# Attention with decay and a gated product on one core: rows of two heads moved by TensorE instead of DMAs in the first four chunks

## The chip, the cores and the metric

The kernel runs on one core of one Trainium2 chip. The metric is the device time in microseconds (us) of one execution. Three runs of the kernel before gave 395.66, 395.9 and 396.56 us, a median of 395.9.

The engines are TensorE (PE; its weight loads are shown as PEld), VectorE (DVE), ScalarE (ACT), GpSimd (POOL) and SyncE (SP), which issues DMAs. Results of PE land in eight PSUM banks.

## The reference

```python
# r, k, v, w: (B=4, H=8, S=768, D=48); u: (H, D)
for t in range(S):
    cur = einsum('bhd,bhe->bhde', u * k[:, :, t], v[:, :, t])
    y[:, :, t] = einsum('bhd,bhde->bhe', r[:, :, t], state + cur)
    state = w[:, :, t, :, None] * state + einsum('bhd,bhe->bhde', k[:, :, t], v[:, :, t])
x = y.transpose(0, 2, 1, 3).reshape(B, S, H * D)
h = maximum(x @ w_in, 0)                      # 384 -> 1024
conv = conv_w[0] * h(t-1) + conv_w[1] * h(t) + conv_w[2] * h(t+1)
out = (h * sigmoid(conv)) @ w_out             # 1024 -> 384
```

The inputs r, k, v, w and u are float32; the three weights of the second part are float64.

## The kernel before

**Tiling.** The sequence of each of the four batches is cut into six chunks of 128 steps, so there are 24 chunks n = 0 to 23, with c = n mod 6. The 384 rows of x are kept transposed in `xT`, as three tiles of 128 partitions, and a high and a low part of each value, so that fast float32r products keep the precision. Three tiles hold eight heads of 48 rows thus: of each tile, rows 0 to 47 and 64 to 111 are a pair of heads, and rows 48 to 63 and 112 to 127 take sixteen rows each of heads 6 and 7. The gaps of the first six heads thus hold the last two heads in three pieces.

**Stage a of a chunk** (`stage_a`) transposes w, k and r on PE with the identity (L517), after an ACT copy that puts heads 6 and 7 into the gaps (L511). Two scans on DVE (L524, L531) make running products of w, and L529 and L535 multiply k and r into them; the result `kr` has k in part 0 and r in part 1. Scores and outputs of heads 6 and 7 need these heads on rows of their own, in `last`: six DMAs on SP's queue (L539) copy sixteen partitions each from `kr` to `last`. POOL makes z = r k u (L543, L545), DVE sums it (L546) and POOL puts the sum on a diagonal (L549). `kback` (L557) transposes k back.

**Stage b** (`stage_b`) makes the scores (L607: for six heads from `kr`, for heads 6 and 7 from `last`), copies their upper half into `pm` (L611), makes the new state (L624, L628), and the outputs: what the state carries (L635, with the decayed state `sd` of L591 and L594 spread by ACT into `sbd`, L599) and what lies within the chunk (L645). ACT and DVE write the outputs as high and low part to `xT` (L651, L653). Heads 6 and 7 land in a spare slot of `xT`; for the chunks c = 3 and c = 5 six DMAs (L662) copy their rows, for all chunks since the last such copy, to the gaps.

**The weights** come in pieces: a DMA load on SP's queue (L455 and L459 for w_in, L470 for w_out), then DVE, ACT and POOL turn float64 into a high and a low float32 part (L419 to L440).

**The blocks.** A block is 384 steps of a batch. For each of eight groups of 128 columns, PE makes x @ w_in (L673), ACT and DVE the gating (L685 to L694), POOL the low part (L695), and PE the output product (L702). A block can start once the chunks that it reads have all rows of their outputs in `xT`; the first block reads chunks 0 to 3.

**The order.** The instructions are not written in the order in which they run. Each step is given to a planner (`Plan.op`) with its engine, a modelled length (`LEN`), what it reads and writes, and a rank. `Plan.issue` goes through modelled time: whenever an engine is free, it takes the ready step with the lowest rank. The order that results is fixed for each engine, and engines run in order on the chip. Loads of chunk n have rank 14 n - 10, its stage a 14 n, its stage b 14 n + 7; the first block starts at rank 56 and its groups are 5 apart; the weight pieces are 4 apart, w_in from 10, w_out from 60. DMAs use one queue, SP's; the planner models what they move.

**The head.** Fourteen products of zeros (L331, `WARM`) run on PE while the first loads are under way. POOL makes the constants and broadcasts u over 128 partitions with one DMA of its own queue (L347).

Of the kernel before, what the change touches and what calls it, by code (L numbers as in the profile page):

```python
# [19 lines left out]
W_LO, W_HI = 0.75, 1.05  # L20
BANKS = 8
GH = 5
WARM = 14

CHUNK, LEAD, UNIT, DOWN, PIECE = 14.0, 0.0, 5.0, 1.6, 4.0
FIRST_IN, FIRST_OUT = 10.0, 60.0
AHEAD, GUARD = 10.0, 10.0
SPREAD = (3, 5)


LEN = dict(
# [2 lines left out]
    stt=0.54, gate=0.47, wts=0.47, wstt=0.47,  # L34
    fill=0.25, kh=0.42, guard=0.72, sbd=0.34, xhi=0.49, relu=0.5, mul=0.49, sig=0.43, cast=0.42, out=0.37, exp=0.52,
    z=0.98, diag=1.07, lo=0.97,
    load=0.55, issue=0.45, spread=0.6,
)
TAIL = dict(PE=0.22, DVE=0.11, ACT=0.13, POOL=0.07, SP=2.2)

# [65 lines left out]
class Plan:  # L106
# [29 lines left out]
    def issue(self):  # L136
        n = len(self.ops)
        left = [len(o[3]) for o in self.ops]
        users = [[] for _ in range(n)]
        for i, o in enumerate(self.ops):  # L140
            for d in o[3]:
                users[d].append(i)
        engines = ("PE", "DVE", "ACT", "POOL", "SP")
        ready = {e: [] for e in engines}
        free = dict.fromkeys(engines, 0.0)
        locked = dict(DVE=0.0, POOL=0.0)
        wire = Wire(("SP", "ACT"))
        for i in range(n):
            if not left[i]:
                ready[self.ops[i][0]].append((self.ops[i][7], i))  # L150
        events, order, t = [], [], 0.0

        def places(bufs):
            taken = []
            for b in bufs:
                if b.t is None:
                    if b.turn == b.kind.served:
                        b.t = b.kind.take()
                    if b.t is None:
                        for x in reversed(taken):  # L160
                            x.kind.places.insert(0, x.t)
                            x.kind.held -= 1
                            x.kind.served -= 1
                            x.t = None
                        return False
                    taken.append(b)
            return True

        while len(order) < n:
            for e in engines:  # L170
                if free[e] > t:
                    continue
                for k, (_, i) in enumerate(sorted(ready[e])):
                    if places(self.ops[i][4]):
                        break
                else:
                    continue
                ready[e].remove((self.ops[i][7], i))
                _, us, _, _, _, moves, port, _ = self.ops[i]
                at = t  # L180
                if port:
                    other = "POOL" if e == "DVE" else "DVE"
                    at = max(t, locked[other])
# [12 lines left out]
            todo = []  # L196
            while events and events[0][0] <= t + 1e-9:
                todo.append(heapq.heappop(events)[1])
            for i in todo:
                if i < 0:  # L200
                    continue
                for b in self.ops[i][4]:
                    b.uses -= 1
                    if not b.uses:
                        b.kind.held -= 1
                        b.kind.places.append(b.t)
                for u in users[i]:
# [81 lines left out]
def rwkv_conv_moe_kernel(  # L289
# [35 lines left out]
    banks = [ps.tile([P, 512], F32, name=f"bank{i}") for i in range(BANKS)]  # L325


    idle = fconst.tile([P, HB], BF16, name="idle")
    nc.vector.memset(idle, 0.0)
    for _ in range(WARM):  # L330
        nc.tensor.matmul(banks[-1][:, 0:HB], lhsT=idle[:, 0:P], rhs=idle, start=True, stop=True)  # L331

# [11 lines left out]
    nc.gpsimd.affine_select(out=upper, in_=ones_f, pattern=[[1, P]], compare_op=ALU.is_gt,  # L344
                            fill=0.0, base=0, channel_multiplier=-1)
    ubc = fconst.tile([P, H, D], F32, name="ubc")
    nc.gpsimd.dma_start(out=ubc, in_=u.rearrange("h d -> (h d)").partition_broadcast(P))  # L347
    cw = const.tile([P, 3, FT], F32, name="cw")
    one_end = fconst.tile([P, WID], F32, name="one_end")
    nc.vector.memset(one_end, 0.0)  # L350
# [30 lines left out]
    kr_k = kind("kr", 3, [P, 2, WID], fill=lambda t: nc.gpsimd.memset(t[:, :, 0:WID:WID - 1], 0.0))  # L381
    last_k = kind("last", 2, [R, 2, SL + 1], fill=lambda t: nc.gpsimd.memset(t, 0.0))
    sbd_k = kind("sbd", 2, [R, NP, R], fill=lambda t: nc.gpsimd.memset(t, 0.0))
    z_k = kind("z", 1, [P, H, D])
    dg_k = kind("dg", 2, [P, H])
    pm_k = kind("pm", 2, [P, 2, NP, L])
    junk_k = kind("junk", 1, [P, H, D], BF16)
    kh_k = kind("kh", 2, [P, NP, R], fill=lambda t: nc.gpsimd.memset(t[:, KT], 0.0))
    sd_k = kind("sd", 2, [R, NP, D])
    s_k = kind("s", 2, [R, NP, D])  # L390
# [89 lines left out]
    def loads(n):  # L480
# [3 lines left out]
        for nm, src in (("w", w), ("k", k), ("r", r), ("v", v)):  # L484
            op("SP", "load", lambda nm=nm, src=src: nc.sync.dma_start(  # L485
                out=st[nm].t[:, :, 0:D], in_=src[b, :, s, :].rearrange("h t d -> t h d")), [], [st[nm]], moves=1.15)

    def seg(t, at):

        return t[:, 0:KT * SL].rearrange("p (m s) -> p m s", s=SL)[:, :, at:at + L] if at == 0 else \  # L490
            t[:, at - 1:at - 1 + KT * SL].rearrange("p (m s) -> p m s", s=SL)[:, :, 1:1 + L]
# [4 lines left out]
    def thirds(t):  # L496
        return t[:, 0:KT * L].rearrange("p (m t) -> p m t", t=L)
# [4 lines left out]
    def stage_a(n):  # L502
# [7 lines left out]
        def tr(src, t, cols):  # L510
# [4 lines left out]
            def f():  # L515
                for m in range(KT):
# [17 lines left out]
        tr(R_, rp, lambda m: rp.t[:, m * L:(m + 1) * L])  # L534
        op("DVE", "kt", lambda: nc.vector.tensor_tensor(out=seg(kr.t[:, 1], 0), in0=thirds(rp.t), in1=seg(kr.t[:, 1], 0),  # L535
                                                        op=ALU.mult), [rp], [(kr, 1)], [kr])
        for g in range(2):
            for m in range(KT):
                op("SP", "spread", lambda g=g, m=m: nc.sync.dma_start(  # L539
                    out=last.t[64 * g + 16 * m:64 * g + 16 * m + 16],  # L540
                    in_=kr.t[64 * g + D:64 * g + 64, :, m * SL:m * SL + SL + 1]), [kr, (kr, 1)], [(last, g, m)], [last],
                    moves=0.05)
        op("POOL", "z", lambda: nc.gpsimd.tensor_tensor(out=z.t, in0=R_.t[:, :, 0:D], in1=K_.t[:, :, 0:D], op=ALU.mult),  # L543
           [R_, K_], [z], port=True)
        op("POOL", "z", lambda: nc.gpsimd.tensor_tensor(out=z.t, in0=z.t, in1=ubc, op=ALU.mult), [], [z], port=True)  # L545
        op("DVE", "dg", lambda: nc.vector.tensor_reduce(  # L546
            out=dg.t.rearrange("p (g m) -> p m g", g=2), in_=z.t.rearrange("p (m g) d -> p m g d", g=2), axis=AX.X,
            op=ALU.add), [z], [dg])
# [20 lines left out]
    def stage_b(n):  # L569
# [13 lines left out]
        def place(m):  # L583

            at = (m + odd) % NP
            return slice(at * L, (at + 1) * L)

        if c:
            sd, sbd = Buf(sd_k), Buf(sbd_k)
            old = chunks[n - 1]["s"]  # L590
            op("DVE", "sd", lambda: nc.vector.tensor_tensor(  # L591
                out=sd.t[:, 0:KT], in0=old.t[:, 0:KT], in1=kr.t[0:R, 0, 1:WID:SL].unsqueeze(2).to_broadcast([R, KT, D]),
                op=ALU.mult), [old, kr], [sd], port=True)
            op("DVE", "small", lambda: nc.vector.tensor_scalar(  # L594
                out=sd.t[:, KT], in0=old.t[:, KT], scalar1=last.t[:, 0, 1:2], scalar2=None, op0=ALU.mult),
                [old, *lasts], [(sd, 1)], [sd, last], port=True)
            for g in range(2):
                p = slice(64 * g, 64 * g + D)
                op("ACT", "sbd", lambda g=g, p=p: nc.scalar.copy(out=sbd.t[p, :, 64 * g:64 * g + D], in_=sd.t[p]),  # L599
                   [sd, (sd, 1)], [sbd] if g == 0 else [(sbd, 1)], [sbd])  # L600
        sc = [Buf(pb), Buf(pb)]

        def scores():
# [10 lines left out]
        if c < NCH - 1:  # L614
# [14 lines left out]
            else:  # L629
                op("DVE", "s", lambda: nc.vector.tensor_copy(out=s.t, in_=tv()[0:R]), [t], [s])  # L630
        y = Buf(pb)
        if c:
            def carried():
                for m in range(NP):
                    nc.tensor.matmul(y.t[0:R, place(m)], lhsT=sbd.t[:, m, :], rhs=rt(m),  # L635
                                     start=(m == 0), stop=False, skip_group_check=True)
            op("PE", "carried", carried, [sbd, (sbd, 1), kr, (kr, 1), *lasts], [y], [last])
# [8 lines left out]
                                     rhs=pm.t[:, g, m, :], start=(c == 0 and m == 0), stop=True,  # L646
                                     skip_group_check=True)
        op("PE", "y", within, [vN, pm, (pm, 0), (pm, 1)], [y])
        ts = slice(1 + c * L, 1 + (c + 1) * L)
        slots = slice(KT * odd, KT * odd + NP)  # L650
        op("ACT", "xhi", lambda: nc.scalar.copy(out=xT[0:R, slots, 0, ts], in_=pairs(y.t)),  # L651
           [y], [("x", odd, c, 0), ("spare", c)])
# [102 lines left out]


    piece = iter([FIRST_IN + PIECE * j for j in range(3 * KT)] + [FIRST_OUT + PIECE * j for j in range(FT)])
    for f0 in range(0, DF, HB):
        plan.rank = FIRST_IN + PIECE * KT * (f0 // HB)
        win_pieces(f0, min(HB, DF - f0), piece)  # L760
        if f0 == 0:
            load_conv()
# [58 lines left out]
```

## Time and profile before

| | |
|---|---|
| three runs, median | 395.9 us (395.66 to 396.56) |
| profiled execution | 397.97 us, of which span 396.3 us |
| PE busy | 353.8 us (89%), 2704 matmuls |
| DVE busy | 279.9 us (71%) |
| ACT busy | 231.6 us (58%) |
| POOL busy | 173.3 us (44%) |
| granted clock of PE, mean | 0.921 |
| DMA | 35.43 MB, mean 89 GB/s; 106640 of 118124 packets under 512 B |
| copies to `last` (L539) | 144 DMAs, 16.2 KB each, median 1.9 us to landing |

The span is the time from the first to the last instruction of the profiled execution. In the strips, the span is cut into forty equal slices, and each digit is the busy share in tenths (PEclk: the clock granted to PE, in tenths of the full one). A row of the timeline has the start and the length of a group of instructions in us, engine, line and operation, the tile written and the tiles read, and, in brackets, the idle time before it and what ended it. SPq is the issuing of DMAs on SP's queue. A line of a helper function can carry several shapes.

### The profile page before, as it was taken

The page shows a single profiled execution, that of the slowest core. Times are in us where ns is not written, and L with a number is a line of the kernel's source. Part 1 is how long each engine was busy: PE and PEld are TensorE (multiplying, and loading weights), DVE is VectorE, ACT ScalarE, POOL GpSimd, SP SyncE. Part 2 cuts the span into 40 slices and gives each one's busy share as a digit, 9 for nine tenths or more (in the row PEclk, how much of TensorE's full clock was granted, in tenths as well). Part 3 has the DMA queues.
Part 4 walks back from the last instruction along what each step waited for, and adds up shares of the span by engine and source line. Part 5 has one row for each costly group of instructions (what it writes and reads, how often), then busy time and mean ns, then how long its engine had stood idle before and what let it go on. Part 6 is the DMA issues. An engine that isn't in the chain of part 4 may idle for free.

```text
span 396.3 us, 7712 instructions
## 1 busy us (share of the span) xinstructions
PE 353.8 (89%) x2704; PEld 320.5 (81%) x2704; DVE 279.9 (71%) x575; ACT 231.6 (58%) x597; POOL 173.3 (44%) x191
## 2 busy tenths in 40 slices
PE   6672485797899999999999999999999999999991
PEld 3561274686888899999899999889899999999991
DVE  4557867879998768678866885688778755746510
ACT  3234445249996666269856663686767526656711
POOL 5418576457774443235554342255444321332320
PEclk9568556679999999999999999999999999999997
DMA  8899996559344254395406443743444221010101
GB/s 151 133 114 153 159 219 168 98 129 120 68 82 91 51 87 88 75 157 90 95 27 110 81 91 72 128 85 84 77 84 86 51 48 54 2 41 22 40 0 66
DMA packets 118124, 35.43 MB, mean 89 GB/s; under 512 B 106640, under 2 KB 115088, under 8 KB 118080
## 3 DMA queue, kind: packets, MB, share of 16 engines
q1 hardware_dynamic: 118016, 34.69, 47.3%
q8 instruction: 23, 0.38, 0.4%
q0 software_dynamic: 64, 0.20, 0.2%
q14 instruction: 21, 0.17, 0.2%
HBM read 25.39 MB, written 4.72 MB: 76 GB/s over the span
## 4 chain that ended last, share of the span: by engine, by line
PE 69%; DMA 10%; DVE 9%; SPq 4%; ACT 3%; issue 2%; POOL 2%; DVEq 0%; POOLq 0%; ACTq 0%
PE bank L702 24%; PE bank L673 21%; PE bank L645 5%; DMA gh<-in_moe_w_in_dram 5%; PE bank L607 5%; PE bank L517 5%; PE bank L635 5%; DMA r<-in_r_dram 4%; SPq L485 3%; PE bank L624 3%; PE bank L557 2%; DVE a L687 1%; DVE a L689 1%; DVE g L692 1%; DVE bank L419 1%
## 5 line engine op out<-in xcount | busy, mean ns | idle before, releaser
L673 PE MATMUL bank<-xT,wi 128*128 128x386 f32 x576 | 127.1, 347 | 2.2 <-DVE val L430 2.2
L702 PE MATMUL bank<-wo,gh 128*128 128x384 f32 x576 | 125.0, 343 | 1.2 <-POOL gh L695 1.2
L695 POOL TENSOR_TENSOR gh<-g,gh 128x384 fp32r<-128x384 f32 x64 | 64.7, 1015 | 122.1 <-ACT gh L694 120.5
L673 PEld LDWEIGHTS bank<-xT,wi 128*128 128x128 f32 x576 | 100.0, 189 | 6.0 <-DVE val L430 2.5
L702 PEld LDWEIGHTS bank<-wo,gh 128*128 128x128 f32 x576 | 100.5, 188 | 2.4 <-POOL gh L695 1.6
L687 DVE SCALAR_TENSOR_TENSOR a<-bank,cw,a 128x384 f32<-128x384 f32 x64 | 38.5, 609 | 14.9 <-ACT a L686 14.8
L691 ACT ACTIVATE a<-a 128x384 f32<-128x384 f32 x64 | 33.3, 522 | 22.5 <-DVE a L689 22.4
L692 DVE TENSOR_TENSOR g<-bank,a 128x384 f32<-128x384 f32 x64 | 34.5, 548 | 16.0 <-ACT a L691 16.0
L611 DVE COPY_PREDICATED pm<-upper,bank 128x512 f32<-128x512 int32 x48 | 33.8, 731 | 12.1 <-PE bank L607 11.9
L685 ACT ACTIVATE bank<-bank 128x386 f32<-128x386 f32 x64 | 30.4, 478 | 17.8 <-PE bank L673 16.7
L549 POOL TENSOR_SCALAR_AFFINE_SELECT pm<-dg 128x1024 f32<-128x1024 f32 x24 | 26.3, 1094 | 33.0 <-PE bank L645 26.8
L694 ACT CAST gh<-g 128x384 fp32r<-128x384 f32 x64 | 32.4, 513 | 13.2 <-DVE g L692 12.9
L689 DVE SCALAR_TENSOR_TENSOR a<-bank,cw,a 128x384 f32<-128x384 f32 x64 | 38.6, 611 | 0.8
L686 ACT ACTIVATE a<-bank,cw 128x384 f32<-128x384 f32 x64 | 36.6, 582 | 0.3
L543 POOL TENSOR_TENSOR z<-r,k 128x384 f32<-128x384 f32 x24 | 24.3, 1013 | 27.0 <-DMA r<-in_r_dram 26.9
L524 DVE TENSOR_TENSOR_SCAN kr<-bank,one_end 128x387 f32<-128x387 f32 x24 | 23.0, 957 | 15.6 <-PE bank L517 15.6
L653 DVE TENSOR_TENSOR xT<-bank,xT 112x512 fp32r<-112x512 f32 x24 | 16.5, 688 | 20.3 <-ACT xT L651 20.1
L645 PE MATMUL bank<-pm,v 128*48 128x128 f32 (+1 forms) x384 | 28.3, 294 | 0.0
L651 ACT CAST xT<-bank 112x512 fp32r<-112x512 f32 x24 | 14.2, 592 | 23.8 <-PE bank L645 23.7
L645 PEld LDWEIGHTS bank<-pm,v 128*48 128x48 f32 (+1 forms) x384 | 21.9, 133 | 5.7 <-issue 3.7
L557 PE MATMUL bank<-ident,kr 128*128 128x128 f32 x72 | 13.9, 308 | 13.5 <-DVE kr L529 13.5
L607 PEld LDWEIGHTS bank<-kr 48*128 48x128 f32 x288 | 20.8, 214 | 6.4 <-issue 4.8
(84 smaller groups left out, 522.8 us busy)
## 6 DMA issues: line engine op xcount, KB each, us to landing
w<-in_w_dram SPq DMA_DIRECT2D x24, 192.0 KB, 3.9
k<-in_k_dram SPq DMA_DIRECT2D x24, 192.0 KB, 4.5
r<-in_r_dram SPq DMA_DIRECT2D x24, 192.0 KB, 4.7
v<-in_v_dram SPq DMA_DIRECT2D x24, 192.0 KB, 3.0
out_dram<-val SPq DMA_DIRECT2D x24, 192.0 KB, 2.0
last<-kr SPq DMA_DIRECT2D x144, 16.2 KB, 1.9
gh<-in_moe_w_out_dram SPq DMA_DIRECT2D x2, 1152.0 KB, 6.6
gh<-in_moe_w_in_dram SPq DMA_DIRECT2D x4, 432.0 KB, 8.2
```

The lines of the kernel that those rows point to most:

```text
L607: nc.tensor.matmul(sc[g].t[:, m * L:(m + 1) * L], lhsT=kt(m)[p], rhs=rt(m)[p], start=True, stop=True)
L611: op("DVE", "cp", lambda g=g: nc.vector.copy_predicated(out=pm.t[:, g], mask=upper.unsqueeze(1).to_broadcast([P, NP, L]), data=sc[g].t.rea ...
L645: nc.tensor.matmul(y.t[rows, cs], lhsT=vf[:, h * D:h * D + rows.stop - rows.start], rhs=pm.t[:, g, m, :], start=(c == 0 and m == 0), stop= ...
L673: nc.tensor.matmul(t.t[:, 0:xs.stop - xs.start], lhsT=wi[:, m, a, f * P:(f + 1) * P], rhs=xT[:, x0 + m, c, xs], start=(m == 0 and j == 0), ...
L686: ("ACT", "mul", lambda: nc.scalar.mul(out=a(), in_=h(1), mul=cw[:, 1, f:f + 1]), [t, "cw"], [a1]),
L687: ("DVE", "stt", lambda: nc.vector.scalar_tensor_tensor(out=a(), in0=h(0), scalar=cw[:, 0, f:f + 1], in1=a(), op0=ALU.mult, op1=ALU.add), ...
L689: ("DVE", "stt", lambda: nc.vector.scalar_tensor_tensor(out=a(), in0=h(2), scalar=cw[:, 2, f:f + 1], in1=a(), op0=ALU.mult, op1=ALU.add), ...
L691: ("ACT", "sig", lambda: nc.scalar.activation(out=a(), in_=a(), func=AF.Sigmoid), [], [a1]),
L692: ("DVE", "gate", lambda: nc.vector.tensor_tensor(out=g.t[:, 0:width], in0=h(1), in1=a(), op=ALU.mult), [t, a1], [g]),
L694: ("ACT", "cast", lambda: nc.scalar.copy(out=part(0)[:, 0:width], in_=g.t[:, 0:width]), [g], [key]),
L695: ("POOL", "lo", lambda: nc.gpsimd.tensor_tensor(out=part(1)[:, 0:width], in0=g.t[:, 0:width], in1=part(0)[:, 0:width].bitcast(F32), op=AL ...
L702: nc.tensor.matmul(acc.t[:, 0:DM], lhsT=part(a)[:, tt * P:(tt + 1) * P], rhs=wo[:, f, c, :], start=(f == 0 and a + c == 0), stop=(f == FT ...
```

## The change

In chunks 0 to 3 (`n < EARLY`), six matmuls with selection matrices `sel` bring the rows of heads 6 and 7 of `kr` into one PSUM bank, and one ACT copy writes them to `last`; the six DMAs are left out there. Also in these chunks, the outputs of heads 6 and 7 are made by PE at their final rows: v of these heads is copied by ACT into a zero-padded `vx`, the decayed state into `sbx`, and the products run over three tiles instead of four pairs. `xT` is written in its final place, and the six DMAs after chunk 3 of the first batch are left out.

u is loaded as one row by SP and broadcast by a product with a row of ones; the second z step now waits for it. `WARM` goes from 14 to 10. The planner counts PE's steps as 1.4 times as long before its time 60 (`COLD`), and a small DMA as 0.64 instead of 0.6.

```diff
-WARM = 14
+WARM = 10
...
+EARLY = 4
+COLD = 60.0
...
+                if e == "PE" and t < COLD:
+                    us *= 1.4
...
-    nc.gpsimd.dma_start(out=ubc, in_=u.rearrange("h d -> (h d)").partition_broadcast(P))
+    sel = fconst.tile([P, KT, R], F32, name="sel")
+    nc.gpsimd.memset(sel, 0.0)
+    for g in range(2):
+        for m in range(KT):
+            nc.gpsimd.tensor_copy(out=sel[:, m, 64 * g + 16 * m:64 * g + 16 * m + 16], in_=ident[:, 64 * g + D:64 * g + 64])
...
+    sbx_k = kind("sbx", 1, [R, KT, P], fill=lambda t: nc.gpsimd.memset(t, 0.0))
+    vx_k = kind("vx", 1, [P, KT, 2, 64], fill=lambda t: nc.gpsimd.memset(t, 0.0))
...
+    def spread_u():
+        t, row = Buf(pa), Buf(val_k)
+        op("SP", "issue", lambda: nc.sync.dma_start(out=row.t[0:1, :], in_=u.rearrange("h d -> (h d)").unsqueeze(0)),
+           [], [row], moves=0.05)
+        op("PE", "gather", lambda: nc.tensor.matmul(t.t[:, 0:H * D], lhsT=ones_f[0:1, :], rhs=row.t[0:1, :],
+                                                    start=True, stop=True), [row], [t])
+        op("ACT", "kh", lambda: nc.scalar.copy(out=ubc.rearrange("p h d -> p (h d)"), in_=t.t[:, 0:H * D]), [t], ["ubc"])
...
+        if n < EARLY:
+            gt = Buf(pa)
+            both = 2 * (SL + 1)
+
+            def gather():
+                for a in range(2):
+                    for m in range(KT):
+                        nc.tensor.matmul(gt.t[0:R, a * (SL + 1):(a + 1) * (SL + 1)], lhsT=sel[:, m, :],
+                                         rhs=kr.t[:, a, m * SL:m * SL + SL + 1], start=(m == 0), stop=(m == KT - 1))
+            op("PE", "gather", gather, [kr, (kr, 1)], [gt])
+            op("ACT", "kh", lambda: nc.scalar.copy(out=last.t.rearrange("p a t -> p (a t)"), in_=gt.t[0:R, 0:both]),
+               [gt], [(last, 0, 0)], [last])
+        else:
...
+        early = n < EARLY
+        if early:
+            vx = Buf(vx_k)
+            op("ACT", "fill", lambda: nc.scalar.copy(
+                out=vx.t[:, :, :, D:64], in_=vN.t[:, 2 * KT:H].rearrange("p g (m i) -> p m g i", m=KT)), [vN], [vx])
...
+                    op("ACT", "sbd", lambda g=g, p=p: nc.scalar.copy(
+                        out=sbd.t[p, 0:KT, 64 * g:64 * g + D], in_=sd.t[p, 0:KT]),
+                        [sd], [sbd] if g == 0 else [(sbd, 1)], [sbd])
+                    op("ACT", "fill", lambda g=g, p=p: nc.scalar.copy(
+                        out=sbx.t[p, :, 64 * g + D:64 * g + 64], in_=sd.t[p, KT].rearrange("p (m i) -> p m i", m=KT)),
+                        [(sd, 1)], [sbx] if g == 0 else [(sbx, 1)], [sbx, sd])
...
+                def carried_rows():
+                    for m in range(KT):
+                        nc.tensor.matmul(y.t[:, m * L:(m + 1) * L], lhsT=sbx.t[:, m, :], rhs=rt(KT),
+                                         start=(m == 0), stop=False, skip_group_check=True)
+                    for m in range(KT):
+                        nc.tensor.matmul(y.t[0:R, m * L:(m + 1) * L], lhsT=sbd.t[:, m, :], rhs=rt(m),
+                                         start=False, stop=False, skip_group_check=True)
...
+            def within_rows():
+                for m in range(KT):
+                    for g in range(2):
+                        nc.tensor.matmul(y.t[64 * g:64 * g + 64, m * L:(m + 1) * L], lhsT=vx.t[:, m, g, :],
+                                         rhs=pm.t[:, g, KT, :], start=(c == 0 and m == 0), stop=False,
+                                         skip_group_check=True)
+                for m in range(KT):
+                    for g in range(2):
+                        nc.tensor.matmul(y.t[64 * g:64 * g + D, m * L:(m + 1) * L], lhsT=vN.t[:, 2 * m + g, :],
+                                         rhs=pm.t[:, g, m, :], start=False, stop=True, skip_group_check=True)
+            op("PE", "y_rows", within_rows, [vx, vN, pm, (pm, 0), (pm, 1)], [y])
+            op("ACT", "kh", lambda: nc.scalar.copy(out=xT[:, 0:KT, 0, ts], in_=thirds(y.t)), [y], [("x", odd, c, 0)])
+            op("DVE", "kt", lambda: nc.vector.tensor_tensor(
+                out=xT[:, 0:KT, 1, ts], in0=thirds(y.t), in1=xT[:, 0:KT, 0, ts].bitcast(F32), op=ALU.subtract),
+                [y, ("x", odd, c, 0)], [("x", odd, c, 1)])
+            return
...
+    plan.rank = -AHEAD + 1
+    spread_u()
```

More of the change, by code (lines that the diff above doesn't have):

```diff
@@ L36 @@
     z=0.98, diag=1.07, lo=0.97,
-    load=0.55, issue=0.45, spread=0.6,
+    gather=1.6, carried_rows=1.4, y_rows=1.5,
+    load=0.55, issue=0.45, spread=0.64,
 )
@@ L325, in rwkv_conv_moe_kernel @@
     banks = [ps.tile([P, 512], F32, name=f"bank{i}") for i in range(BANKS)]
-    idle = fconst.tile([P, HB], BF16, name="idle")
-    nc.vector.memset(idle, 0.0)
+    junk = fconst.tile([P, H, D], BF16, name="junk")
+    nc.vector.memset(junk, 0.0)
+    idle = junk.rearrange("p h d -> p (h d)")
     for _ in range(WARM):
@@ L386, in rwkv_conv_moe_kernel @@
     pm_k = kind("pm", 2, [P, 2, NP, L])
-    junk_k = kind("junk", 1, [P, H, D], BF16)
+    junk_k = Kind(1, ([junk], []))
     kh_k = kind("kh", 2, [P, NP, R], fill=lambda t: nc.gpsimd.memset(t[:, KT], 0.0))
@@ L536, in stage_a @@
                                                         op=ALU.mult), [rp], [(kr, 1)], [kr])
[L537 to L542, printed above, removed]
+        if n < EARLY:
[12 more added lines that the diff above has]
+                for m in range(KT):
+                    op("SP", "spread", lambda g=g, m=m: nc.sync.dma_start(
+                        out=last.t[64 * g + 16 * m:64 * g + 16 * m + 16],
+                        in_=kr.t[64 * g + D:64 * g + 64, :, m * SL:m * SL + SL + 1]), [kr, (kr, 1)], [(last, g, m)],
+                        [last], moves=0.05)
         op("POOL", "z", lambda: nc.gpsimd.tensor_tensor(out=z.t, in0=R_.t[:, :, 0:D], in1=K_.t[:, :, 0:D], op=ALU.mult),
            [R_, K_], [z], port=True)
-        op("POOL", "z", lambda: nc.gpsimd.tensor_tensor(out=z.t, in0=z.t, in1=ubc, op=ALU.mult), [], [z], port=True)
+        op("POOL", "z", lambda: nc.gpsimd.tensor_tensor(out=z.t, in0=z.t, in1=ubc, op=ALU.mult), ["ubc"], [z], port=True)
         op("DVE", "dg", lambda: nc.vector.tensor_reduce(
@@ L586, in place @@
             return slice(at * L, (at + 1) * L)
+        early = n < EARLY
[3 more added lines that the diff above has]
+                out=vx.t[:, :, :, D:64], in_=vN.t[:, 2 * KT:H].rearrange("p g (m i) -> p m g i", m=KT)), [vN], [vx])
         if c:
             sd, sbd = Buf(sd_k), Buf(sbd_k)
+            if early:
+                sbx = Buf(sbx_k)
             old = chunks[n - 1]["s"]
@@ L598, in stage_b @@
                 p = slice(64 * g, 64 * g + D)
-                op("ACT", "sbd", lambda g=g, p=p: nc.scalar.copy(out=sbd.t[p, :, 64 * g:64 * g + D], in_=sd.t[p]),
-                   [sd, (sd, 1)], [sbd] if g == 0 else [(sbd, 1)], [sbd])
+                if early:
+                    op("ACT", "sbd", lambda g=g, p=p: nc.scalar.copy(
[4 more added lines that the diff above has]
+                        [(sd, 1)], [sbx] if g == 0 else [(sbx, 1)], [sbx, sd])
+                else:
+                    op("ACT", "sbd", lambda g=g, p=p: nc.scalar.copy(out=sbd.t[p, :, 64 * g:64 * g + D], in_=sd.t[p]),
+                       [sd, (sd, 1)], [sbd] if g == 0 else [(sbd, 1)], [sbd])
         sc = [Buf(pb), Buf(pb)]
@@ L631, in stage_b @@
         y = Buf(pb)
+        ts = slice(1 + c * L, 1 + (c + 1) * L)
+        if early:
+            if c:
+                def carried_rows():
[5 more added lines that the diff above has]
+                                         start=False, stop=False, skip_group_check=True)
+                op("PE", "carried_rows", carried_rows, [sbd, (sbd, 1), sbx, (sbx, 1), kr, (kr, 1), *lasts], [y], [last])
+            def within_rows():
[4 more added lines that the diff above has]
+                                         skip_group_check=True)
+                for m in range(KT):
+                    for g in range(2):
+                        nc.tensor.matmul(y.t[64 * g:64 * g + D, m * L:(m + 1) * L], lhsT=vN.t[:, 2 * m + g, :],
[6 more added lines that the diff above has]
+            return
         if c:
@@ L648, in stage_b @@
         op("PE", "y", within, [vN, pm, (pm, 0), (pm, 1)], [y])
-        ts = slice(1 + c * L, 1 + (c + 1) * L)
         slots = slice(KT * odd, KT * odd + NP)
```

## The prediction

> **What bounds the kernel now.** I read the page's strips of forty slices first, then the windows.
>
> ```profile
> PE   6672485797899999999999999999999999999991
> PEclk9568556679999999999999999999999999999997
> ```
> ```profile
> 0.00:26.00 26.00, 17.96 (x102) 12.09 (x102) 12.04 (x32) 7.74 (x22) 9.84 (x26) 0.74 0.84 124
> 26.00:66.00 40.00, 21.53 (x137) 16.16 (x136) 31.67 (x72) 18.26 (x53) 24.67 (x28) 0.63 0.99 163
> 66.00:90.00 24.00, 20.73 (x162) 18.03 (x163) 18.52 (x42) 11.35 (x33) 13.47 (x14) 0.69 0.60 149
> 90.00:122.00 32.00, 28.31 (x209) 26.00 (x209) 30.44 (x63) 28.89 (x76) 24.96 (x26) 1.00 0.50 85
> 122.00:388.00 266.00, 265.10 (x2097) 248.14 (x2095) 187.09 (x369) 164.85 (x416) 100.35 (x99) 1.00 0.37 70
> ```
>
> The columns of the windows are length, then busy time of PE, PE's weight load, DVE, ACT and POOL, then granted clock, DMA share and GB/s. Four stages appear. From 122 to 388 PE is busy 265.10 of 266 us, so whatever happens earlier only shifts this part. From 90 to 122 DVE is the fullest engine (30.44 of 32). From 66 to 90 nothing is full: DVE rests 5.48 us, PE 3.27, and PE's clock is 0.69. From 26 to 66 the DMA share is 0.99 and PE rests 18.47 us. So a saving counts if it brings DMA's work forward before 66, or lets DVE work between 66 and 90; PE time as such is free before 66.
>
> Now the SyncE queue (SPq), in the timeline, with the chain of waits' two DMA steps behind it:
>
> ```profile
> 9.26 1.12 SPq L455 DMA_DIRECT2D gh<-in_moe_w_in_dram  x1
> 10.43 0.44 SPq L459 DMA_DIRECT2D gh<-in_moe_w_in_dram  x1
> 10.99 4.16 SPq L539 DMA_DIRECT2D last<-kr  x6
> 16.89 0.32 SPq L455 DMA_DIRECT2D gh<-in_moe_w_in_dram  x1
> 17.80 3.77 SPq L539 DMA_DIRECT2D last<-kr  x6
> 23.32 1.48 SPq L485 DMA_DIRECT2D w<-in_w_dram  x1
> ```
> ```profile
> 9.26 7.61 DMA gh<-in_moe_w_in_dram
> 17.25 5.99 DMA gh<-in_moe_w_in_dram
> ```
> ```profile
> 16.00:18.00 2.00, 0.21 (x3) 0.15 (x1) 0.00 (x0) 0.00 (x0) 0.65 (x1) 0.50 0.18 31
> 22.00:24.00 2.00, 1.28 (x13) 1.08 (x12) 0.67 (x2) 0.66 (x2) 0.00 (x0) 0.80 0.53 30
> ```
>
> The issue at 16.89 is the 17th on this queue; the 9th, at 9.26, lands at 16.87. The load at 23.32 is the 26th; the 18th, at 17.25, lands at 23.24. Both fit one reading: an issue waits for the landing of the one eight before it. Six small copies of kr therefore use up six of eight places, and each time the DMA engines run dry: share 0.18 in 16 to 18, 0.53 in 22 to 24.
>
> **The change part by part.** *Queue.* Twelve copies of chunks 0 and 1 leave the queue ahead of chunk 2's loads (one tiny load of u joins it). Counted by eights, chunk 2's w becomes the 15th issue and waits only for chunk 1's k, so the second half of the first weight piece and chunk 2's loads stand in the queue before the engines run dry. The two holes are worth 2 x (1 - 0.18) = 1.64 and 2 x (1 - 0.53) = 0.94 us, together 2.6. As the share is 0.99 afterwards, I let all 2.6 us through to 66. The bounds are 0, if another wait opens the same holes, and 2.6 plus the room left by the copies themselves, for which I add nothing.
>
> *Chunks 2 and 3.* These rows carry their path.
>
> ```profile
> 41.20 0.55 DVE L535 TENSOR_TENSOR kr<-bank,kr 128x384 f32<-128x384 f32 x1
> 44.36 5.34 SPq L539 DMA_DIRECT2D last<-kr  x6
> 50.79 1.30 PE L607 MATMUL bank<-last 48*128 48x128 f32 x4 [0.17 <-DMA last<-kr]
> 54.15 0.55 DVE L535 TENSOR_TENSOR kr<-bank,kr 128x384 f32<-128x384 f32 x1
> 59.01 4.62 SPq L539 DMA_DIRECT2D last<-kr  x6
> 67.23 1.65 PE L607 MATMUL bank<-kr 48*128 48x128 f32 x12
> 72.80 1.66 PE L645 MATMUL bank<-pm,v 128*48 128x128 f32 x16
> 75.84 3.79 SPq L662 DMA_DIRECT2D xT<-xT  x6
> 85.33 3.46 PE L673 MATMUL bank<-xT,wi 128*128 128x386 f32 x18
> ```
>
> Chunk 2's kr is whole at 41.75 and its last rows are used at 50.79, 9.0 us later, because the copies stand behind loads in SPq. Chunk 3's is whole at 54.70, and its scores run at 67.23, 12.5 us later. Its outputs are made at 74.46 and copied to their final rows until 79.63, and the first block's products start at 85.33.
>
> *What PE gets.* Per chunk: six products of 129 columns and one ACT copy; six carried products for four; twelve products of outputs for eight. Two matmul records make one such product. The nearest rows, at half and at full clock:
>
> ```profile
> 78.11 1.66 PE L607 MATMUL bank<-kr 48*128 48x128 f32 x12
> 88.72 0.94 PE L607 MATMUL bank<-kr 48*128 48x128 f32 x12
> 81.84 1.49 PE L635 MATMUL bank<-kr,sbd 112*112 112x128 f32 x6
> 83.12 0.63 PE L635 MATMUL bank<-last,sbd 112*112 112x128 f32 x2
> 35.13 0.44 ACT L559 COPY kh<-bank 128x336 f32<-128x336 f32 x1 [0.19 <-PE bank L557]
> 60.28 0.69 DVE L653 TENSOR_TENSOR xT<-bank,xT 112x512 fp32r<-112x512 f32 x1 [3.42 <-ACT xT L651]
> ```
>
> The gather costs 1.66 at half clock (0.94 at full), the carried part half of 1.49 + 0.63, so 1.06, the outputs half of 1.66, so 0.83. That is 3.55 us a chunk at half clock, and 4 x 2.49 + 3 x 1.06 = 13.1 us in all, since chunk 0 carries nothing. Cover: PE's 18.47 us of rest in 26 to 66 for chunks 2 and 3, and 8.04 us in 0 to 26 for 0 and 1. Without that cover it would be 13.1 on the path.
>
> New path of chunk 3: kr whole at 54.70, gather 1.66 and copy 0.44, then scores to outputs as now, 74.46 - 67.23 = 7.2, plus 1.06 + 0.83. That is 65.9, less the 2.6 of the queue, 63.3; the cast and the subtraction (0.6 and 0.55) give about 64.5 where 85.33 stood. The first block could start 20 us earlier. PE can use that: it is slowed and idle there. DVE decides how much is kept: gating work that now comes after 85 moves into its rests of 66 to 90, 5.48 us. In 90 to 122 DVE still rests 1.56 of 32, 4.9%; I leave this share open in 24 us as well, 1.2, and count 0.55 for four subtractions of 128x384 (0.55, as L535) for four of 112x512 (0.69). Sum: 5.48 - 1.2 + 0.55 = 4.8 us; bounds 0 and 6.0. ACT gets per chunk the copy of 0.44 and four small ones, against 0.1 saved on the cast; it is busy 11.35 of 24 us, so I price it at nothing.
>
> *Head.* POOL loses the u broadcast and gets memsets and six small copies, ahead of its first z at 7.78; its rest before that z covers them:
>
> ```profile
> 7.78 1.00 POOL L543 TENSOR_TENSOR z<-r,k 128x384 f32<-128x384 f32 x1 [3.29 <-DMA r<-in_r_dram]
> 1.20 4.66 PE L331 MATMUL bank<-idle 128*128 128x384 bf16 x14 [1.20 <-DVE table L335]
> 6.90 0.55 PE L517 MATMUL bank<-ident,k 128*128 128x128 f32 x3 [0.70 <-ACT k L511]
> 10.70 0.91 PE L517 MATMUL bank<-ident,w 128*128 128x128 f32 x3 [0.84 <-ACT w L511]
> ```
> ```profile
> L383 POOL MEMSET sbd<- 112x448 f32 x2 | 0.9, 476 | 0.0
> ```
>
> Three memsets of at most 384 columns are bounded by 3 x 0.48 = 1.4 us and six copies of 16 columns by as much again, less than the rest of 3.29. The second z now waits for u, which is loaded fifth on SPq and then passes PE and ACT; behind that z POOL has chunk 0's diagonal, which is needed only at chunk 0's copy of the scores. I price it at zero, at most one z's length, 1.0. Ten warming products for fourteen end 1.3 us sooner, but the next transposes wait for k at 6.90 anyway: zero. If PE is then still slow, three groups of transposes cost 0.36 more each (0.91 against 0.55), 1.1 us, on a chunk that does not set the end. I take zero; the range keeps 1.1.
>
> The Trainium skill, TensorE: Matmul & The Clock Gate, Part 1, "The HAM clock gate", speaks against this last edit: the clock rises only after a sustained busy window of about 3.4 us, and ten products of 0.33 us last barely one. By that rule the sum would lose those 1.1 us; the trace agrees so far as the fourteen are followed by fast transposes at 6.90 and slow ones at 10.70, once PE has rested.
>
> Total: 2.6 + 4.8 = 7.4 us. The profiled execution had a span of 396.3 and a time of 397.97, 1.67 around it: the span becomes 388.9 and its time 390.6. The median of the runs, 395.9, lies 2.1 below that execution; taking off the same 7.4 gives 388.5.
>
> **The rivals.** *Only the queue.* The order on each engine is written again from modelled lengths; DVE is in order, and one wrongly placed instruction holds the others. For it:
>
> ```profile
> 40.27 0.56 DVE L419 TENSOR_SCALAR bank<-gh 128x384 int32<-128x384 int32 x1 [3.10 <-DMA gh<-in_moe_w_in_dram]
> ```
>
> Here DVE waited 3.10 us for weights while chunk 2's last kr step (41.20, above) stood behind. If new waits replace the 4.8, only 2.6 is left: 393.3.
>
> *Nothing.* The stage of 90 to 122 is as long as the conversion of the output weights lasts, and if their loads come no earlier, the end doesn't move: 395.9. Against it: the last of these loads is issued behind loads that themselves wait for chunk 4.
>
> *More.* An earlier chunk 2 also fills half of DVE's rest of 26 to 66 (40 - 31.67 = 8.33): 7.4 + 4.2 = 11.6, so 384.3. Against it: the DMA share there is 0.99.
>
> *Slower.* PE executes in order, so the gather and the longer outputs of chunks 2 and 3 may stand ahead of the transposes and scores that DVE waits for, at half clock. Price: 2 x 3.55 = 7.1 us, less the wait that they replace:
>
> ```profile
> PE bank L607 <- DMA last<-kr: 4.0, 4, 1.8
> ```
>
> That leaves +3.1 us: 399.0. It decides if PE is full from 41 to 66 and the first block's product comes no sooner than 85.33 + 3. For it: only 4.0 us of PE's waiting is laid to these copies; against it: PE's rest of 18.47 us.
>
> **How the numbers follow.** Forecast 0.46, only the queue 0.18, more 0.12, nothing 0.08, slower 0.16. Under 0.2% (0.8 us) a measurement of this kernel can't tell a difference. Faster: 0.46 + 0.18 + 0.12 = 0.76; same 0.08; slower 0.16. The range reaches from somewhat beyond "more" to just over "nothing": 382.5 to 397.0, which leaves out nearly all of "slower" and some 0.04 below.
>
> **What would show it.** Right: no dry DMA window between 16 and 24; chunk 2's w issued before 17; the first L673-like product before 70 (its line number moves); DVE over 90% busy from 66 to 90; full clock from about 75 on instead of 84; PE again without gaps to the end, which comes 7 us sooner. Wrong: the first block's product after 80, new DVE waits of 3 us and more between 30 and 66, or PE gaps after 122.

## The result and the profile after

The kernel after ran in 386.2 us (median of four runs, 383.68 to 387.25) against 395.78 us of the kernel before beside it: a ratio of 0.9752, interval 0.9716 to 0.9788; by that ratio it is 9.8 us less (8.4 to 11.2). The profiled execution took 386.26 us, its span is 384.3, 12.0 shorter than before; the profiled execution before lies 2.1 us above the median of its runs, so the traces show somewhat more than the 9.8. The forecast was 388.5 us, 7.4 less.

The strips of forty slices, after:

```profile
PE   7747788899899999999999999999999999999992
PEclk9978689989899999999999999999999999999997
```

PE's digits are 8 or 9 from the sixth slice on (but for the last), before from the eleventh. The windows, with the same cuts as before (length; busy PE, PE's weight load, DVE, ACT, POOL; clock, DMA share, GB/s):

```profile
0.00:26.00 26.00, 16.39 (x107) 11.32 (x107) 13.47 (x34) 10.62 (x33) 12.89 (x37) 0.97 0.99 154
26.00:66.00 40.00, 31.11 (x280) 26.69 (x280) 38.81 (x87) 23.91 (x73) 28.25 (x31) 0.81 0.86 195
66.00:90.00 24.00, 21.96 (x171) 19.73 (x173) 22.86 (x47) 19.75 (x54) 17.34 (x18) 0.93 0.32 63
90.00:122.00 32.00, 29.64 (x234) 26.50 (x229) 28.30 (x59) 21.41 (x57) 20.99 (x22) 0.95 0.39 81
```

Read DVE's column against before: 13.47 for 12.04, 38.81 for 31.67, 22.86 for 18.52, 28.30 for 30.44. That is 10.8 us more of DVE's time used by 122. Not all of it is more work: over the whole execution DVE's 575 instructions take 284.4 us where 575 took 279.9, mostly the two steps that decay the state (L633 and L636, 10.3 and 9.4 us; before, L591 and L594, 8.1 and 5.7). What counts for the end is what is left at 122: for DVE 6.3 us less (180.9 for 187.2), and for PE, which rests nearly nowhere from there on, 10.1 us less (255.2 for 265.3). The largest part of DVE's gain, 7.1 us, lies in 26 to 66, where it now rests 1.2 us of 40. The conversion of the last weight piece ends nearly 12 us sooner, first before, then after:

```profile
111.58 0.54 DVE L430 SCALAR_TENSOR_TENSOR val<-gh,bank 128x384 f32<-128x384 uint32 x1
```
```profile
99.81 0.54 DVE L444 SCALAR_TENSOR_TENSOR val<-gh,bank 128x384 f32<-128x384 uint32 x1
```

The DMA column changed too: in 26 to 66 the share fell from 0.99 to 0.86 while the rate rose from 163 to 195 GB/s.

The queue of SyncE in the timeline, where the loads are issued:

```profile
9.70 0.43 SPq L459 DMA_DIRECT2D conv<-in_moe_conv_w_dram  x1
10.25 8.26 SPq L499 DMA_DIRECT2D w<-in_w_dram  x1
18.68 1.06 SPq L499 DMA_DIRECT2D k<-in_k_dram  x1
36.75 4.82 SPq L484 DMA_DIRECT2D gh<-in_moe_w_out_dram  x2
53.57 0.53 SPq L484 DMA_DIRECT2D gh<-in_moe_w_out_dram  x1
66.64 4.35 SPq L574 DMA_DIRECT2D last<-kr  x6
```

Chunk 2's w is offered at 10.25 instead of 23.32, with no copy ahead of it; its issue lasts 8.26 us, to 18.51. The first output weights are asked for at 36.75, in the kernel before at 51.78 (L470); the last third at 53.57 instead of 84.95:

```profile
51.78 0.78 SPq L470 DMA_DIRECT2D gh<-in_moe_w_out_dram  x1
64.31 0.58 SPq L470 DMA_DIRECT2D gh<-in_moe_w_out_dram  x1
84.95 0.58 SPq L470 DMA_DIRECT2D gh<-in_moe_w_out_dram  x1
```

PE's timeline has the first block and the new products:

```profile
10.69 3.33 PE L566 MATMUL bank<-kr,sel 128*112 128x130 f32 x12 [0.80 <-DVE kr L551]
42.12 1.64 PE L566 MATMUL bank<-kr,sel 128*112 128x130 f32 x6 [0.86 <-DVE kr L557]
53.34 0.83 PE L566 MATMUL bank<-kr,sel 128*112 128x130 f32 x6
54.93 0.92 PE L566 MATMUL bank<-kr,sel 128*112 128x130 f32 x6 [0.75 <-DVE kr L557]
65.32 0.42 PE L750 MATMUL bank<-xT,wi 128*128 128x386 f32 x1
66.21 4.33 PE L750 MATMUL bank<-xT,wi 128*128 128x386 f32 x23 [0.47 <-DVE xT L706]
```

A gather, twelve records, costs 3.33 us at half clock and up to two times 0.92 at full, twice what the prediction took for each. The first block's first product comes at 65.32 instead of 85.33, the next at 66.21.

### The profile page after: what moved, and what is told of

The parts are those of the page before. It is cut to its first block, busy times and chain, and to the rows that moved or that the text cites. A ratio compares the mean times of both kernels' runs of the same rounds, so it can differ in the third digit from the quotient of the medians.

```text
span 384.3 us, 7880 instructions
## 1 busy us (share of the span) xinstructions
PE 354.3 (92%) x2794; PEld 323.7 (84%) x2794; DVE 284.4 (74%) x575; ACT 234.7 (61%) x612; POOL 174.5 (45%) x199
## 4 chain that ended last, share of the span: by engine, by line
PE 77%; DVE 12%; issue 2%; DMA 2%; SPq 2%; POOL 2%; ACT 1%; DVEq 0%; ACTq 0%; POOLq 0%
PE bank L779 26%; PE bank L750 25%; PE bank L657 6%; PE bank L723 5%; PE bank L539 5%; PE bank L713 4%; PE bank L674 3%; PE bank L592 2%; SPq L499 2%; PE bank L566 1%; DVE kr L546 1%; DVE kr L553 1%; DMA r<-in_r_dram 1%; DVE e L438 1%; DVE bank L441 1%
## 5 line engine op out<-in xcount | busy, mean ns | idle before, releaser
L750 PE MATMUL bank<-xT,wi 128*128 128x386 f32 x576 | 125.7, 347 | 0.5 <-DVE xT L706 0.5
L750 PEld LDWEIGHTS bank<-xT,wi 128*128 128x128 f32 x576 | 101.2, 190 | 3.3 <-issue 2.2
L771 ACT CAST gh<-g 128x384 fp32r<-128x384 f32 x64 | 32.1, 511 | 10.7 <-DVE g L769 10.4
L809 ACT COPY val<-bank 128x384 f32<-128x384 f32 x24 | 11.6, 482 | 25.9 <-PE bank L779 24.4
L580 POOL TENSOR_TENSOR z<-z,ubc 128x384 f32<-128x384 f32 x24 | 24.3, 1013 | 3.9 <-ACT ubc L508 2.9
L657 PEld LDWEIGHTS bank<-kr 48*128 48x128 f32 x288 | 19.5, 198 | 6.5 <-issue 4.9
L657 PE MATMUL bank<-kr 48*128 48x128 f32 x288 | 24.4, 302 | 0.4 <-DVE g L769 0.4
L553 DVE TENSOR_TENSOR_SCAN kr<-bank,dA 128x387 f32<-128x387 f32 x24 | 22.8, 952 | 0.0
L723 PE MATMUL bank<-pm,v 128*48 128x128 f32 x320 | 21.8, 279 | 0.0
## 6 DMA issues: line engine op xcount, KB each, us to landing
last<-kr SPq DMA_DIRECT2D x120, 16.2 KB, 1.8
```

Source lines behind the costliest of these rows:

```text
L657: nc.tensor.matmul(sc[g].t[:, m * L:(m + 1) * L], lhsT=kt(m)[p], rhs=rt(m)[p], start=True, stop=True)
L723: nc.tensor.matmul(y.t[rows, cs], lhsT=vf[:, h * D:h * D + rows.stop - rows.start], rhs=pm.t[:, g, m, :], start=(c == 0 and m == 0), stop= ...
L750: nc.tensor.matmul(t.t[:, 0:xs.stop - xs.start], lhsT=wi[:, m, a, f * P:(f + 1) * P], rhs=xT[:, x0 + m, c, xs], start=(m == 0 and j == 0), ...
L771: ("ACT", "cast", lambda: nc.scalar.copy(out=part(0)[:, 0:width], in_=g.t[:, 0:width]), [g], [key]),
```

## The experiments

**Theory A**: six small copies per chunk stand in SP's in-order queue and wait there for kr; the loads behind them, of chunks and weights, come late, and DVE, which converts the weights and feeds every chunk, rests. Off the queue, DVE is full from 26 to 107 and sets the pace. **Rivals**: B, the planner's new lengths make a better order; C, the outputs at their final rows count, since they let the first block start early; and, for the cost, that the products of PE lie on the path. Each kernel ran beside the kernel before on the same chip; ratios are to it.

**The planner's lengths alone**, in the kernel before:

```diff
+                if e == "PE" and t < COLD:
+                    us *= 1.4
...
-    load=0.55, issue=0.45, spread=0.6,
+    load=0.55, issue=0.45, spread=0.64,
```

> The kernel before with only the planner's new lengths (PE's steps 1.4 times as long before its time 60, a small DMA 0.64 instead of 0.6); nothing that is computed or moved changes. Theory A (the copies off SP's queue and the earlier first block let DMA and DVE work without rests): this order brings little, 392 to 398 us, since the six copies per chunk still stand ahead of the loads. Theory B (the gain comes from a better order through better lengths): 389 us or less.

393.37 us, ratio 0.9921 (0.9878 to 0.9964). This lies in the range of theory A: the lengths alone gain 3.1 us, more than nothing, and less than a third of the whole. The first output weights are still issued at 54.22. B is not the main cause, but it is a part of the change that the prediction had not priced.

**Without the planner's lengths**, in the kernel after:

```diff
-                    us *= 1.4
+                    us *= 1.0
...
-    load=0.55, issue=0.45, spread=0.64,
+    load=0.55, issue=0.45, spread=0.6,
```

> The kernel after with the planner's old lengths (PE's early steps not stretched, a small DMA 0.6). Theory A: the removal of the copies makes the gain and the lengths bring 0 to 3 us of it, 386 to 389 us. Theory B: 391 us or more.

390.47 us, ratio 0.9869 (0.9792 to 0.9946): 1.2% above the kernel after's 0.9752, some 4.6 us. With the old lengths the rest of the change gains 1.3%, with the old kernel the lengths gain 0.8%, and together they gain 2.5%. The interval reaches into the ranges of both theories. A stands in its main part, but its expectation of 386 to 389 was missed: I had given the lengths at most 3 us. Its first block starts at 62.64, earlier than in the kernel after, and still it is slower.

**Only the gather**; outputs of heads 6 and 7 as before, with the six DMAs after chunk 3:

```diff
-        early = n < EARLY
+        early = False
```

> The kernel after, with the outputs of heads 6 and 7 made as before: in the spare slot, with six DMAs to the final rows after chunk 3. Only the gather replaces the copies to last. Theory A with the queue as its main part: most of the gain stays, 386 to 390 us, and the first block starts some 6 us later than after. Theory C (the outputs at their final rows are what lets the first block start early): 391 us or more.

385.03 us, ratio 0.9692 (0.9649 to 0.9735), as fast as the whole change or a little faster, and just below the range of theory A. The timeline of this kernel:

```profile
38.05 4.08 SPq L484 DMA_DIRECT2D gh<-in_moe_w_out_dram  x1
43.95 3.93 SPq L484 DMA_DIRECT2D gh<-in_moe_w_out_dram  x2
65.87 4.40 SPq L739 DMA_DIRECT2D xT<-xT  x6
73.76 2.28 PE L750 MATMUL bank<-xT,wi 128*128 128x386 f32 x6
```

and its window:

```profile
66.00:90.00 24.00, 19.64 (x140) 16.39 (x141) 22.94 (x50) 16.19 (x45) 18.43 (x19) 0.86 0.51 100
```

The first block starts 8.4 us later than in the kernel after, and nothing is lost: DVE is as full in 66 to 90 (22.94 against 22.86), with weights instead of gating. C falls as the main cause: the start of the first block does not set the time.

**Only the final rows**; the six copies per chunk in place of the gather:

```diff
-        if n < EARLY:
+        if False:
             gt = Buf(pa)
```

> The kernel after, with the six DMAs per chunk to last instead of the gather; outputs at their final rows as after. Theory A: SP's queue is held by the copies again, the first w_out load is issued near 50 instead of 37, and 391 to 396 us result. Theory C (final rows): 386 to 389 us.

390.18 us, ratio 0.9839 (0.9793 to 0.9886), between the ranges of A and C. The first block starts at 72.55, about as early as with the gather alone, yet 1.5% is missing. The copies stand in the queue, and the output weights come at 51.64, 63.21 and 72.86:

```profile
20.11 7.82 SPq L574 DMA_DIRECT2D last<-kr  x12
43.15 4.96 SPq L574 DMA_DIRECT2D last<-kr  x6
51.64 2.12 SPq L484 DMA_DIRECT2D gh<-in_moe_w_out_dram  x1
56.12 5.79 SPq L574 DMA_DIRECT2D last<-kr  x6
```

Two things here do not fit a simple picture. Chunk 2's w is issued at 10.66, about as early as in the kernel after, since the planner now puts it ahead of the copies; so an early w is no sign that the copies are gone, and it alone does not bring the gain. And with all copies in place this kernel is still 0.8% faster than the one with the planner's lengths alone (0.9921); the intervals just touch, and no run tells whether the final rows or the new head bring it.

**The gather, and copies on the queue all the same.** This tells the place on the queue from the time until `last` is there. Six DMAs per chunk wait for kr and write into a part of xT that nobody reads before it is written again; this work is added, and nothing waits for its data.

```diff
             op("ACT", "kh", lambda: nc.scalar.copy(out=last.t.rearrange("p a t -> p (a t)"), in_=gt.t[0:R, 0:both]),
                [gt], [(last, 0, 0)], [last])
+            for g in range(2):
+                for m in range(KT):
+                    op("SP", "spread", lambda g=g, m=m: nc.sync.dma_start(
+                        out=xT[64 * g + 16 * m:64 * g + 16 * m + 16, KT, :, 1 + n * L:1 + (n + 1) * L].bitcast(F32),
+                        in_=kr.t[64 * g + D:64 * g + 64, :, m * SL:m * SL + L]), [kr, (kr, 1), ("spare", n)],
+                        [("hold", n, g, m)], moves=0.05)
```

> The kernel after, gather and all, but in chunks 0 to 3 six DMAs per chunk of nearly the size of the old copies stand on SP's queue again, waiting for kr as those did; they write into a part of xT that nobody reads before batch 1 overwrites it. Scores and outputs do not wait for them. Theory A in the form that only the place on SP's queue matters: loads stand behind them as before, the first w_out load is issued at 48 or later, and 389 to 394 us result. Rival (what counts is that last is there sooner): no more than 387.5 us.

394.88 us, ratio 0.9991 (0.9959 to 1.0022), just above the range given: the whole gain is gone, though `last` comes from PE as in the kernel after. The first output weights come at 44.55, not at 48 or later. Its queue and its window:

```profile
20.41 4.56 SPq L573 DMA_DIRECT2D xT<-kr  x6
25.09 0.51 SPq L499 DMA_DIRECT2D r<-in_r_dram  x1
36.87 3.83 SPq L573 DMA_DIRECT2D xT<-kr  x6
44.55 4.34 SPq L484 DMA_DIRECT2D gh<-in_moe_w_out_dram  x2
48.99 4.09 SPq L573 DMA_DIRECT2D xT<-kr  x6
54.08 0.37 SPq L499 DMA_DIRECT2D r<-in_r_dram  x1
61.10 4.17 SPq L573 DMA_DIRECT2D xT<-kr  x6
```
```profile
26.00:66.00 40.00, 26.90 (x233) 22.95 (x234) 32.25 (x77) 20.80 (x63) 25.18 (x28) 0.72 0.75 161
```

DVE rests 7.8 us again in 26 to 66. The chunks' loads (r at 25.09 and 54.08) stand right behind copies that nobody waits for. So the added copies are enough to take the gain away; the sooner finished `last` alone does not keep it. There are three limits. The planner knows of the added DMAs, so the order of other steps changed with them. The copies also read kr, so its buffers can come free later, and the run does not tell this from the place on the queue. And why the kernel with the final rows, whose copies are as many, is 1.5% faster than this one is not settled: by 122 DVE worked 98.8 us there and 94.0 here (92.7 in the kernel before), though the output weights are asked for first at 51.64 there and at 44.55 here, so the place of that one load does not decide.

**The copies on another queue**, in the kernel before:

```diff
-                op("SP", "spread", lambda g=g, m=m: nc.sync.dma_start(
+                op("ACT" if n < 4 else "SP", "spread", lambda g=g, m=m: (nc.scalar if n < 4 else nc.sync).dma_start(
```

> The kernel before, with the 24 copies to last of chunks 0 to 3 issued by ACT on its own queue instead of SP's; the copies, their bytes and their time to land remain, and ACT pays some 3.6 us of issuing per chunk. Theory A in its sharp form (the copies hurt because loads stand behind them on SP's queue): the first w_out load is issued near 37 to 42 instead of 52, and 385 to 391 us result. Rival (what counts is the time the copies themselves take until last is there): 393 us or more.

410.9 us, ratio 1.0367 (1.0315 to 1.0418), slower. It lies in the range of the rival, which had no upper end, but not for the rival's reason; the timeline of ACT shows what happens:

```profile
7.83 0.27 ACT L511 COPY r<-r 128x96 f32<-128x96 f32 x1 [1.73 <-DMA r<-in_r_dram]
17.01 10.38 ACTq L539 DMA_DIRECT2D last<-kr  x6
27.43 0.44 ACT L559 COPY kh<-bank 128x336 f32<-128x336 f32 x1 [19.33 <-DMA last<-kr]
```

ACT computes nothing for 19.33 us: it waits some 9 us before the first copy, the six copies of chunk 0 take 10.38 us to issue, 4.16 on SP's queue before, and all of ACT's work stands behind. (The issues of chunks 1 to 3 sum to 3.7 to 4.6 us a chunk, near the 3.6 expected.) The queue was moved, not emptied. SP's first loads do come early (chunk 2's w at 12.47), but the first output weights come at 56.04, later than before, so the run does not tell theory A from its rival; it shows only that the engine which issues such copies pays for them.

**PE's price: each gather done twice**, in the same order:

```diff
-                for a in range(2):
+                for a in (0, 1, 0, 1):
```

> The kernel after with each gather done twice in the same PSUM bank (24 matmul records for 12); the order on all engines is the same. Theory A: DVE sets the pace from 26 to 105, PE has rests there, and the repeated products cost 0 to 1.5 us in all. Rival: the gather lies on the path of each chunk, and four repeats of 0.8 to 1.6 us cost 4 to 6 us.

388.01 us, ratio 0.9773 (0.9714 to 0.9833), against 0.9752 and 0.9733 (below) of the kernel after: 0.8 to 1.6 us more, within the noise of both. The gather's matmuls went from 10.1 to 20.5 us:

```profile
L566 PE MATMUL bank<-kr,sel 128*112 128x130 f32 x48 | 10.1, 365 | 11.8 <-DVE kr L557 6.6 <-DVE kr L551 5.2
```
```profile
L566 PE MATMUL bank<-kr,sel 128*112 128x130 f32 x96 | 20.5, 393 | 11.0 <-DVE kr L551 6.8 <-DVE kr L557 3.9
```

**DVE's price: one step of each weight conversion done twice**, in the same order:

```diff
-        op("DVE", "wts", lambda: nc.vector.tensor_scalar(
-            out=mant(), in0=word(1), scalar1=0xfffff, scalar2=0x100000, op0=ALU.bitwise_and, op1=ALU.bitwise_or),
-            reads, [y])
+        def mantissa():
+            for _ in range(2):
+                nc.vector.tensor_scalar(
+                    out=mant(), in0=word(1), scalar1=0xfffff, scalar2=0x100000, op0=ALU.bitwise_and, op1=ALU.bitwise_or)
+        op("DVE", "wts", mantissa, reads, [y])
```

> The kernel after, with one DVE step of the conversion of the 17 weight pieces done twice; the order on all engines is the same. That is about 14 x 0.46 + 3 x 0.33 = 7.4 us more of DVE, nearly all before 107. Theory A (DVE is full from 26 to 107 and sets the pace): 5 to 8 us slower than the kernel after, 391 to 394 us. Rival (PE's or the DMAs' pace): 0 to 2 us.

392.16 us, ratio 0.9911 (0.9875 to 0.9947): 1.6 to 1.8% above the kernel after, 6.3 to 7.0 us. The step in the kernel after and in this one, for the pieces of 384 columns:

```profile
L441 DVE TENSOR_SCALAR bank<-gh 128x384 int32<-128x384 int32 x14 | 7.6, 546 | 0.0
```
```profile
L443 DVE TENSOR_SCALAR bank<-gh 128x384 int32<-128x384 int32 x28 | 15.5, 554 | 0.5
```

DVE is busy 292.3 us for 284.4, 7.9 us more. Ten us on PE cost about one, eight on DVE six to seven. In the kernel after DVE is busy 78.6 of the 81 us from 26 to 107; there it sets the pace.

**The kernel after once more**

> The kernel after once more, unchanged, beside the other runs of this call: 384 to 388 us.

386.0 us, ratio 0.9733 (0.9672 to 0.9795).

**u's product ranked later**

```diff
-                                                    start=True, stop=True), [row], [t])
+                                                    start=True, stop=True), [row], [t], rank=0.5)
```

(and its ACT copy likewise).

> The kernel after, with the product that broadcasts u and its ACT copy ranked behind chunk 0's transposes; the load of u stays where it is. Theory A (DVE is full from 26 on and its work is set by what the weights' loads bring): chunk 0's first transposes come about 2 us earlier, the time changes by 0 to -1.5 us against the kernel after. Rival (chunk 0's start is on the path): -2 us or more.

386.38 us, ratio 0.9757 (0.9705 to 0.9808). Inconclusive: the planner still put the product first (it starts at 6.68, chunk 0's transposes at 8.23), so the edit did not do what it was for.

**The old head with the gather only**: outputs as before, u broadcast by POOL, fourteen warming products:

```diff
-WARM = 10
+WARM = 14
...
+    nc.gpsimd.dma_start(out=ubc, in_=u.rearrange("h d -> (h d)").partition_broadcast(P))
...
-    spread_u()
...
-        early = n < EARLY
+        early = False
```

> Only the gather of the change (and the planner's lengths): outputs as before with six DMAs after chunk 3, u broadcast by POOL, fourteen warming products, no memsets for sbx and vx. Theory A: the queue is free in the head and the gather does the rest, 383 to 387 us, as good as the kernel after. Rival (final rows and u's product carry 3 us or more): 389 us or more.

386.64 us, ratio 0.9754 (0.9701 to 0.9808), the kernel after's time. Here chunk 0's transposes start at 5.63 and are fast:

```profile
5.63 0.49 PE L539 MATMUL bank<-ident,w 128*128 128x128 f32 x3
```

In the kernel after they start at 7.71 and are slow:

```profile
7.71 0.90 PE L539 MATMUL bank<-ident,w 128*128 128x128 f32 x3
```

Two us at chunk 0's start are worth nothing that can be measured.

This kernel also gives the cleanest price of the copies: it differs from the one with the planner's lengths alone (0.9921, 0.9878 to 0.9964) only by the gather in place of the copies (and by a scratch tile that two uses share). That is 1.7%, some 6.6 us, and the intervals are apart.

**The change for six chunks**

```diff
-EARLY = 4
+EARLY = 6
```

> The change for chunks 0 to 5 instead of 0 to 3, so that the whole first batch uses neither copies nor the DMAs to the final rows. Theory A: chunks 4 and 5 lie where PE is no longer free (2 x 1.9 us at full clock at most) but the queue is freed of 18 more DMAs; as DVE is full there, 0 to 3 us slower than the kernel after. Rival (every copy off the queue gains): 2 us or more faster, 384 us or less.

384.77 us, ratio 0.9753 (0.9678 to 0.9829): neither better nor worse; by the ratio this is the lower edge of theory A's range, and the rival's is missed. The 18 further DMAs off the queue do not gain, since from chunk 4 on the weights' loads are already out, and their price on PE does not show either. No kernel here is shown to beat the kernel after; the gather alone equals it with less code.

## Why the prediction was right, step by step

**The number.** 388.5 forecast, 386.2 measured. The direction was right, and so were the two places named, DMA's work before 66 and DVE's rests after it; that the sum is off by no more than 2.3 us is in part luck, since its terms were off both ways.

**The start of the first block**: 64.5 forecast, 65.32 measured (66.21 for all but one product). The path, gather and copy instead of the wait behind the queue, was right, but the closeness is luck. The forecast took chunk 3's kr as whole 2.6 us sooner, at 52.1. It was whole at 54.88, no sooner than before (54.70), and chunk 2's at 42.07 (before 41.75):

```profile
41.52 0.55 DVE L557 TENSOR_TENSOR kr<-bank,kr 128x384 f32<-128x384 f32 x1
54.33 0.55 DVE L557 TENSOR_TENSOR kr<-bank,kr 128x384 f32<-128x384 f32 x1
```

From there to the first product the forecast counted 12.4 us, with rows at half clock; it took 10.4, since PE's products for chunk 3 ran at full speed (the second half of the gather 0.92 us, twelve records of scores 0.94).

**DVE between 66 and 90**: 4.8 forecast, of which 4.3 by filled rests; 4.34 measured. The size was right, the cause only in part. I put it down to gating moved forward by the early block. The gather alone fills the same rests to 22.94 with a block that starts at 73.76. What fills them is any work that is ready, and the weights were.

**The queue**: 2.6 us, the step that failed, in size and in what it would bring. It counted two dry windows of chunks 0 and 1, let their 2.6 us through to 66 as sooner chunks, and took a DMA share of 0.99 after 26 for a full resource. The window after shows 195 GB/s at a share of 0.86, where before it was 163 at 0.99, so a high share was no bound. Chunks 2 and 3 came no sooner, as their kr shows; the weights did (output weights 15 to 31 us, the last conversion nearly 12). The copies of chunks 2 and 3, at 44.36 and 59.01, had k, r, v and output weights behind them. By 66 DVE had used 8.6 us more (1.4 in 0 to 26 and 7.1 in 26 to 66), part of it in longer steps; the rival "more" counted 4.2 of DVE's rest in 26 to 66. In 90 to 122 2.1 us were given back, as less was left to do there. And the limit of eight issues was not the only one: chunk 2's w is the 15th issue, as counted, but the issue itself lasts 8.26 us.

**PE's price**: the gather was costed at 1.66 and takes 3.33 at half clock. The row chosen, the scores, has products of 48 rows of the array, and twelve of them take half the time of twelve with 112 or 128 rows; the carried products, (1.49 + 0.63) / 8 records x 12 = 3.2, were the nearer row. Since PE rests there, the doubled gather shows the error to cost nearly nothing, and the rival "slower" has no ground: it needed PE full from 41 to 66, and PE is busy 21.32 of these 25 us.

**The planner's lengths** were a source of mishaps in the prediction, not of gain. Alone they bring 3.1 us, and without them 4.6 us of the change is missing. With the 6.6 us of the gather on top of the lengths, the 3.1 add up to 9.7, the whole gain; the lengths, which the forecast left out, are thus a large part of why it fell short of 9.8.

**The head**: zero was right. The transposes did run at half speed after ten warming products (3.38 us of work; 0.90 for three transposes) and at full after fourteen in the old head (4.58 us; 0.49). The rule of the Trainium skill (TensorE: Matmul & The Clock Gate, Part 1, "The HAM clock gate"), that about 3.4 us of sustained work are needed, agrees with both. After the ten PE also rested 1.59 us before u's product, which the runs do not tell from the smaller number. Neither shows in the time.

**The signs named in advance**: chunk 2's w before 17 (10.25, but the kernel with the final rows shows it with all copies in place), the block before 70 (65.32), DVE over 90% in 66 to 90 (95%), PE without gaps after 122 (253.88 of 254 us to 376) and an end that moves by 7 us or more (12.0) came. Between 16 and 24 the DMA share stays at 0.78 or above, but 53 and 80 GB/s in 16 to 20 are hardly a full queue. PE's clock is not full throughout from 75 on (0.93 and 0.95 in the two windows). No new wait of DVE of 3 us came between 30 and 66.

## What to carry to other kernels

On a queue that issues in order, a small transfer that waits for computed data can hold up every load behind it; count what stands behind it, to the last stage that is fed, not only the moments when the DMA engines run dry. To find what such a gap is worth, look at which engine does the work that the delayed loads bring, and sum its rests over all stages until another engine takes over. Here an engine with rests was charged ten us for about one; the engine that set the pace paid six to seven for eight.

## What was not expected of the hardware

The clock that the profile grants reads 1.00 for the first 24 us of the kernel after, while three transposes take 0.90, 0.85 and 0.85 us at 7.71 to 9.04 and 0.49 later: before its first change, that column can't be trusted, and the durations of equal instructions are the better clock. Products with 48 rows of the array took half the time per record of those with 112 or 128 (1.66 against 3.33 for twelve at half clock). Six copies of 16.2 KB once took 10.38 us to issue from ACT beside the loads of SP (3.7 to 4.6 in the three chunks that followed), and 4.16 from SP itself. The mean busy share of the DMA engines was lower when they moved more: 0.86 at 195 GB/s, 0.99 at 163. Two DVE steps of the same shapes and number, those that decay the state, took 10.3 and 9.4 us in all in one kernel and 8.1 and 5.7 in the other; why, the runs do not show.
